# Sums of factor weights moved behind the product of their step, in a fused attention and two-layer kernel on one core

## Chip, core and metric

The kernel runs on one core of a Trainium2 chip. The metric is the device time of one execution in microseconds (us): a median of 858.5 us over three runs (857.91 to 858.9). The profile that is quoted here is of one more execution, which took 857.15 us.

Engines by their names in the profile: PE is TensorE (matmuls; PEld its weight loads), DVE is VectorE, ACT is ScalarE, POOL is GpSimd, SP is SyncE, which here only issues DMAs. Each engine works through its own list of instructions in the order of the program. ACT and POOL issue DMAs from their own lists too.

## The reference

Attention in which a query sees only the keys of its hash bucket, and behind it a layer with a squared ReLU:

```
q_bits, k_bits = (q @ proj > 0), (k @ proj > 0)          # 6 bits: a bucket number
mask   = q_bucket[:, :, :, None] == k_bucket[:, :, None, :]
scores = where(mask, (q @ k.T) / sqrt(64), -1e9)
x      = softmax(scores) @ v                             # 4 x 8 heads, 768 x 64
x      = x as 3072 tokens x 512
out    = max(x @ w_in, 0) ** 2 @ w_out                   # 512 -> 2048 -> 512
```

All in float32.

## The kernel before

**Stages.** The attention comes first, in pairs of heads, up to about 317 us of the profile; beside it the two weight matrices are converted, cut into blocks, and written back to DRAM. What follows is the layer, in three chunks of 1024 tokens. For each chunk there is a hidden stage (`hidden` for the first chunk, `hidden_pair` for the others) and an output stage (`project`). The tokens stand on the free axis, so the hidden values of a chunk are kept in SBUF as five big tiles `b11`, `b12`, `b21`, `b22`, `b_t`.

**Fast matrix products.** Both products of the layer are computed with seven products of half-sized blocks instead of eight (Winograd's form). The blocks of weights enter as sums and differences, prepared once; the blocks of activations as sums and differences made by VectorE (`minus`). The output product is cut twice so: `project` runs over seven outer products, k = 0 to 6, and each is a call of `product` (L828), which does seven inner ones. The chunks after the first also cut three of their seven hidden products once more (`inner_steps`); the weights for this are the *factors* in the DRAM tile `w_in_49`, and they are made while the first chunk is computed.

**One call of `product`** issues seven blocks of four matmuls of 128x256 in the output stage. The weights of each block are a `leaf`, loaded by ACT's queue. Three accumulators in PSUM (`acc0` to `acc2`, two buffers each) take the results. Intermediate states are copied out by ACT (`one`, `two`, `five`, `three`, L844). The finished results are taken by four callbacks `c11`, `c12`, `c22`, `c21`, mostly additions on VectorE (`add_to`, L1201) that read PSUM. Behind the second block stands a `hook` (L1340): it changes a quarter of this product's activations in place (L1342; the seventh block reads the result) and, for some k, makes the activation sums of the next product (`inner_sums`, L1171). In products 4, 5 and 6, finished blocks of the output are transposed on VectorE (`put_out`, L1215) into a tile of the tag `h` and written to the output by four DMAs each, on SyncE's queue or GpSimd's.

**The factors.** `factor_units(n)` (L953), n = 0 to 3, runs in the first chunk's output stage alone, once ahead of each of the products k = 1 to 4:

```
src = [new_h()... for _ in range(2)]          # two tiles, loaded on GpSimd's queue (L957)
sums = [new_h()... for _ in range(2)]         # two tiles, four VectorE instructions (L586 to L589)
...                                           # two stores into w_in_49 on GpSimd's queue (L964)
```

The four VectorE instructions are `sums_a` (L585): one addition and three subtractions of 128x256. The tiles come from `new_h` (L918): `p_r.tile([P, HN], FP32, name="h", bufs=NH)`, with NH = 5 buffers of 128x512 for all tiles of the tag `h`, those of `put_out` among them. A tile takes a buffer when it is asked for, and its first writer waits until whatever used the buffer is done.

**What sets the order.** The layer is written under a manual schedule: on each engine the instructions stand as the code calls them, and waits are put in for data and for buffers. So the place of a call in `project` is the place of its instructions in each engine's list. Between the products stand further sums: after k = 0 and k = 2 two large differences and `inner_sums` (L1367, L1373), after k = 3 and 4 two differences of the next chunk's x (`sum_x`, L1362). On GpSimd's queue the next chunk's x is loaded at k = 0, then come the factors' loads and stores, at k = 5 two pairs of `raw_qk` loads (L879).

Of the kernel before, what the change touches and what calls it, by code (L numbers as in the profile page):

```python
# [34 lines left out]
def kernel(  # L35
# [45 lines left out]
    HF, HD, NR, NQ = DFF // 2, DM // 2, NFF // 2, NFF // 4  # L81
# [503 lines left out]
    def sums_a(a11, a12, a21, a22, s1, s2, s3, s4):  # L585
        nc.vector.tensor_tensor(out=s1, in0=a21, in1=a22, op=ALU.add)  # L586
        nc.vector.tensor_tensor(out=s3, in0=a11, in1=a21, op=ALU.subtract)
        nc.vector.tensor_tensor(out=s2, in0=s1, in1=a11, op=ALU.subtract)
        nc.vector.tensor_tensor(out=s4, in0=a12, in1=s2, op=ALU.subtract)  # L589
# [31 lines left out]
    for pr in range(NIN, NP):  # L621
        n = 16 if pr == NP - 1 else 1 + (pr % 3 == 0)
# [4 lines left out]
    def load_x(i, fs=slice(0, NFT)):  # L627

        if i not in xs:
            x = p_c.tile([P, NFT, NCH], FP32, name="x")  # L630
            xs[i] = x, [p_c.tile([P, 2, NCH // 2], FP32, name=f"t_x{n}") for n in range(3)]
        nc.gpsimd.dma_start(out=xs[i][0][:, fs], in_=x_all[:, fs, i * NCH:(i + 1) * NCH])
# [23 lines left out]
    with tc.manual_schedule():  # L656
# [261 lines left out]
        def new_h():  # L918
            return p_r.tile([P, HN], FP32, name="h", bufs=NH)
# [30 lines left out]

        thirds = {}

        def factor_units(n):  # L953

            src = [new_h().rearrange("p (a f c) -> p a f c", a=2, c=P) for _ in range(2)]
            for j in range(2):
                nc.gpsimd.dma_start(out=src[j], in_=w_in_7[j * NQ + n, :, 5:7])  # L957
            sums = [new_h().rearrange("p (a f c) -> p a f c", a=2, c=P) for _ in range(2)]
            sums_a(
                src[0][:, :, 0], src[0][:, :, 1], src[1][:, :, 0], src[1][:, :, 1],  # L960
                *(sums[j // 2][:, :, j % 2] for j in range(4)),
            )
            for m in range(2):
                nc.gpsimd.dma_start(out=w_in_49[n, :, 0:2, 2 * m:2 * m + 2], in_=sums[m])  # L964
# [232 lines left out]
        def block(t, n):  # L1197
            return t[:, n]

        def add_to(out, one, two):  # L1200
            nc.vector.tensor_tensor(out=out, in0=one, in1=two, op=ALU.add)  # L1201

        def whole(one, two):

            if two is None:
                return one
            t = p_y.tile([P, QN], FP32, name="tmp", bufs=2)
            add_to(t, one, two)
            return t

        def put_out(i, ih, jh, n, o):


            ot = p_r.tile([P, HN], FP32, name="h", bufs=NH)
            nc.vector.transpose(out=ot, in_=o)  # L1215
            m0 = ih * HD + n * P
            at = slice(i * NCH + jh * HN, i * NCH + (jh + 1) * HN)
            for a in range(P // 32):
                queue = nc.gpsimd if (ih, jh) == (1, 1) else nc.sync
                queue.dma_start(  # L1220
                    out=out[at, m0 + a * 32:m0 + (a + 1) * 32].rearrange("(c i) j -> i c j", i=32),
                    in_=ot[a * 32:(a + 1) * 32].rearrange("i (c j) -> i c j", j=32),
                )
# [37 lines left out]
        def project(i):  # L1261

            V, W, U, X = (p_y.tile([P, 4, QN], FP32, name=f"sum{n}") for n in range(4))
            outs = {}

            def out_block(ih, jh, n):

                row, col = n // 2, n % 2
                if (ih, jh, row) not in outs:
                    outs[ih, jh, row] = [p_y.tile([P, HN], FP32, name="o", bufs=NOUT), 0]  # L1270
                o = outs[ih, jh, row]
                return o[0][:, col * QN:(col + 1) * QN]

            def close(ih, jh, n):
                o = outs[ih, jh, n // 2]
                o[1] += 1
                if (i, ih, jh) == (NCHUNK - 1, 1, 0):
                    put = put_last if n == 2 else put_part
                    put(n, o[0][:, n % 2 * QN:(n % 2 + 1) * QN])
                elif o[1] == 2:  # L1280
                    put_out(i, ih, jh, n // 2, o[0])

            def first_(n, one, two):
                if two is None:
                    nc.scalar.copy(out=block(V, n), in_=one)
                else:
                    add_to(block(V, n), one, two)

            def seventh(n, one, two):
                add_to(block(W, n), block(V, n), whole(one, two))  # L1290

            def fifth(n, one, two):
                if two is None:
                    nc.scalar.copy(out=block(U, n), in_=one)
                else:
                    add_to(block(U, n), one, two)

            def third(n, one, two):
                add_to(block(X, n), block(U, n), whole(one, two))
                add_to(block(X, n), block(X, n), block(V, n))  # L1300

            def second(n, one, two):
                add_to(out_block(0, 0, n), block(V, n), whole(one, two))
                close(0, 0, n)

            def sixth(n, one, two):
                t = whole(one, two)
                add_to(out_block(0, 1, n), block(X, n), t)
                close(0, 1, n)
                add_to(block(W, n), block(W, n), t)  # L1310
                add_to(out_block(1, 1, n), block(W, n), block(U, n))
                close(1, 1, n)

            def fourth(n, one, two):
                add_to(out_block(1, 0, n), block(W, n), whole(one, two))
                close(1, 0, n)

            more = i + 1 < NCHUNK
            uses = first_, seventh, fifth, third, second, sixth, fourth
            for k in range(7):  # L1320
                b = OUTER[k][1]
                t1, t2 = tens.pop(k)
                if k == 0 and more:
                    load_x(i + 1)
                if i == 0 and 0 < k <= NQ:
                    factor_units(k - 1)
                if i == 0 and k == NQ + 1:
                    load_peak(0)
                    load_peak(1)
                if k >= 5 and more:  # L1330
                    load_inner(i + 1, 0, (k - 5,))
                at = lambda m, k=k: lambda n: leaves[k, m][:, n]
                bt = {
                    "11": lambda n: b[:, n, 0:QN], "21": lambda n: b[:, NQ + n, 0:QN],
                    "22": lambda n: b[:, NQ + n, QN:HN], "t1": lambda n: t1[:, n],
                    "t2": lambda n: t2[:, n], "t3": lambda n: b[:, n, QN:HN],
                    "t4": lambda n: b[:, NQ + n, 0:QN],
                }

                def hook():  # L1340
                    y21 = b[:, NQ:NR, 0:QN]
                    minus(y21, y21, t2)  # L1342
                    if k + 1 < 7 and k not in (1, 3):
                        inner_sums(k + 1)
                    if k == 6 and more:
                        load_third_inner(i + 1, 0, nc.scalar)
                        sums_inner(i + 1)

                counted = []

                def a_with_load(m, k=k):
                    load_leaf(7 * k + len(counted) + NLEAF - 2)
                    counted.append(m)
                    return at(m)

                use = uses[k]
                product(
                    NQ, QN, a_with_load, bt, lambda *p: use(0, *p), lambda *p: use(1, *p),
                    lambda p: use(2, p, None), lambda *p: use(3, *p), hook,
                    (i, k) == (NCHUNK - 1, 6),  # L1360
                )
                if k in (3, 4) and i + 1 < NCHUNK:  # L1362
                    sum_x(i + 1, 2 * k - 5)
                    sum_x(i + 1, 2 * k - 4)
                if k == 4 and i + 1 == NCHUNK:
                    guard()
                if k == 0:  # L1367

                    for h in range(2):
                        at_h = slice(h * NQ, (h + 1) * NQ)  # L1370
                        minus(b11[:, at_h], b22[:, at_h], b_t[:, at_h])
                    inner_sums(2)
                if k == 2:  # L1373

                    for h in range(2):
                        at_h = slice(h * NQ, (h + 1) * NQ)
                        minus(b_t[:, at_h], b21[:, at_h], b11[:, at_h])
                    inner_sums(4)
# [291 lines left out]
```

## Time and profile before

| what | value |
|---|---|
| median of three runs | 858.5 us (857.91 to 858.9) |
| the profiled execution: its time, its span | 857.15 us, 855.6 us |
| granted clock of TensorE | 0.999 |
| first chunk's output stage | about 413.7 to 498.3 us |
| busy in it: PE, DVE, ACT, POOL | 84.6, 77.1, 11.7, 18.4 us |
| in product 2 alone (437.9 to 450.0): PE, DVE | 12.1, 8.1 us |
| loads of factors (`h<-w_in`, 8): issue to landing | 4.7 to 13.1 us, median 6.7 |
| stores of factors (`w_in<-h`, 8): issue to landing | 3.2 to 6.5 us, median 4.4 |
| output writes (`out_dram<-h`, 88): issue to landing | 1.8 to 5.1 us, median 3.6 |

The span is the time from the first to the last instruction of the profiled execution; its own time holds 1.55 us more. Times inside the profile count from the span's start. A timeline row gives start, length, engine, source line, operation, tiles written and read, shapes; in brackets the idle time of the engine before it and what ended it. A row of the chain gives start and length of a piece of the work that set the end. The profile leaves buffer numbers out of tile names, so `h` stands for all tiles of that tag, `b` for four of the five big ones.

### The profile page before, as it was taken

Reading aid. Unit: us, or ns where it says so; the run is one execution under the profiler, and the core shown is the slowest. Engines: PE = TensorE matmul, PEld = TensorE weight load, DVE = VectorE, ACT = ScalarE, POOL = GpSimd, SP = SyncE. Lnnn points to the kernel's source line nnn. Section 1 sums busy time; section 2 is a strip of 40 time slices with the busy share of each in tenths; the row PEclk is TensorE's granted clock in tenths of the full one; section 3 lists DMA queues with packets and bytes.
Section 4 is the critical chain, followed back from the end, with each engine's and each line's share of the span. In section 5 each row is a group of like instructions: output and inputs, shape, how many; then the busy total and the mean of one; then the engine's idle time right before and its main releaser. Section 6 shows DMA issues by size and latency. Waiting matters only on the chain.

```text
span 855.6 us, 16996 instructions
## 1 busy us (share of the span) xinstructions
PE 847.3 (99%) x6593; PEld 527.2 (62%) x6593; DVE 749.2 (88%) x1026; ACT 402.0 (47%) x752; POOL 167.8 (20%) x281
## 2 busy tenths in 40 slices
PE   8999999999999999999999999999999999999998
PEld 3544444444544444444788865657888765668886
DVE  5899999999999987989889978888889788889776
ACT  5887777788877762222211135554111355541110
POOL 1321111113321100653121121111000211200003
PEclk9999999999999999999999999999999999999999
DMA  9766899879999525999977976437657875335467
GB/s 201 137 146 152 178 183 200 196 165 249 250 230 230 169 69 214 327 319 291 363 240 221 269 182 221 164 114 276 197 150 190 182 245 172 124 119 161 140 174 144
DMA packets 235892, 170.12 MB, mean 199 GB/s; under 512 B 169320, under 2 KB 192944, under 8 KB 235808
## 3 DMA queue, kind: packets, MB, share of 16 engines
q1 hardware_dynamic: 194832, 87.78, 40.8%
q0 software_dynamic: 16512, 42.45, 15.8%
q10 hardware_dynamic: 24464, 38.78, 15.0%
q8 instruction: 53, 0.87, 0.4%
q14 instruction: 31, 0.25, 0.1%
HBM read 127.14 MB, written 41.16 MB: 197 GB/s over the span
## 4 chain that ended last, share of the span: by engine, by line
PE 97%; DMA 1%; DVE 1%; ACT 0%; issue 0%; SPq 0%; ACTq 0%; DVEq 0%
PE acc L837 39%; PE st L429 18%; PE xo L484 15%; PE acc L1099 13%; PE acc L1052 8%; PE tot L533 2%; PE hash L359 1%; DMA out_dram<-h 1%; DMA qk_nat<-in_k_dram 1%; DVE o L1201 0%; DVE h L1215 0%; DVE h L1232 0%; DVE tmp L1201 0%; DVE bits L409 0%; DVE sum L1201 0%; PE xo L359 0%
## 5 line engine op out<-in xcount | busy, mean ns | idle before, releaser
L435 ACT ACTIVATE e<-st 128x768 f32<-128x768 f32 x192 | 155.5, 810 | 58.3 <-PE st L429 55.2
L429 PE MATMUL st<-feat 64*64 64x384 f32 x1536 | 157.4, 483 | 1.0 <-DVE feat L328 1.0
L484 PE MATMUL xo<-e,v_nat 64*64 64x385 f32 (+1 forms) x1520 | 157.1, 483 | 0.0
L837 PE MATMUL acc<-b,leaf 128*128 128x256 f32 x600 | 133.1, 379 | 0.0
L837 PEld LDWEIGHTS acc<-b,leaf 128*128 128x128 f32 x600 | 113.8, 190 | 16.1 <-issue 0.7
L472 DVE TENSOR_TENSOR total<-total,e 128x1536 f32<-128x1536 f32 x64 | 111.7, 1746 | 4.2 <-ACT e L435 2.8
L395 POOL DMA_DIRECT2D bits<-signed x120 | 62.2, 522 | 217.3 <-ACT signed L384 198.8
L484 PEld LDWEIGHTS xo<-e,v_nat 64*64 64x64 f32 (+1 forms) x1520 | 56.3, 133 | 67.4 <-issue 58.9
L1099 PE MATMUL acc<-t_x,w_unit 128*128 128x512 f32 x192 | 91.0, 596 | 0.0
L429 PEld LDWEIGHTS st<-feat 64*64 64x64 f32 x1536 | 56.0, 133 | 39.2 <-issue 33.8
L837 PE MATMUL acc<-t,leaf 128*128 128x256 f32 x336 | 75.9, 379 | 0.0
L837 PEld LDWEIGHTS acc<-t,leaf 128*128 128x128 f32 x336 | 63.8, 190 | 8.7
L914 DVE SCALAR_TENSOR_TENSOR b<-h 128x512 f32<-128x512 f32 x96 | 65.7, 691 | 3.0
L429 PE MATMUL st<-bits 64*64 64x384 bf16 x768 | 64.9, 325 | 0.1
L837 PE MATMUL acc<-x,w_unit 128*128 128x512 f32 x128 | 56.5, 593 | 0.0
L837 PE MATMUL acc<-b_t,leaf 128*128 128x256 f32 x240 | 53.8, 379 | 0.0
L844 ACT COPY two<-acc 128x256 f32<-128x256 f32 (+1 forms) x29 | 12.5, 432 | 87.8 <-PE acc L837 66.1
L1099 PEld LDWEIGHTS acc<-t_x,w_unit 128*128 128x128 f32 x192 | 35.7, 190 | 27.1 <-issue 23.0
L1220 POOL DMA_DIRECT2D out_dram<-h x24 | 15.6, 657 | 182.1 <-DVE h L1215 182.1
L837 PEld LDWEIGHTS acc<-b_t,leaf 128*128 128x128 f32 x240 | 45.6, 190 | 6.2
L844 ACT COPY one<-acc 128x256 f32<-128x256 f32 (+1 forms) x29 | 12.5, 432 | 78.2 <-PE acc L837 59.0
L429 PEld LDWEIGHTS <-bits 64*64 64x64 bf16 x768 | 23.7, 107 | 37.5 <-issue 36.4
(178 smaller groups left out, 1288.3 us busy)
## 6 DMA issues: line engine op xcount, KB each, us to landing
leaf<-w_out ACTq DMA_DIRECT2D x142, 256.0 KB, 3.1
raw<-in_moe_w_in_dram SPq DMA_DIRECT2D x8, 1024.0 KB, 6.8
raw<-in_moe_w_out_dram SPq DMA_DIRECT2D x8, 1024.0 KB, 7.5
w_unit<-w_in SPq DMA_DIRECT2D x16, 512.0 KB, 4.0
w_unit<-w_in SPq DMA_DIRECT2D x8, 896.0 KB, 8.7
w_out<-sums POOLq DMA_DIRECT2D x16, 448.0 KB, 8.2
v_nat<-in_v_dram SPq DMA_DIRECT2D x16, 384.0 KB, 5.2
x_all<-x_t SPq DMA_DIRECT2D x16, 384.0 KB, 3.0
```

Of the source, the lines that this page charges most:

```text
L395: nc.gpsimd.dma_start(out=t[h * D:h * D + NBITS + 1, w, c * HS:(c + 1) * HS], in_=signed[at:at + NBITS + 1, h],)
L429: nc.tensor.matmul(out=st[k * HK:(k + 1) * HK, h, 0:HS], lhsT=src[1][rows, key], rhs=src[0][rows, cut], start=first, stop=not first, skip_ ...
L435: nc.scalar.activation(out=key_of(pr, kt)[:, :, i, 0:HS], in_=st[:, :, 0:HS], func=ACTF.Exp, scale=scale)
L472: nc.vector.tensor_tensor(out=totals[pr], in0=totals[pr], in1=e, op=ALU.add)
L484: return nc.tensor.matmul(out=outs[pr][h * D:(h + 1) * D, c, 0:HS + 1], lhsT=nat[pr, "v_nat"][rows, h, kt * D:(kt + 1) * D], rhs=key_of(pr ...
L533: done = nc.tensor.matmul(out=spares[pr][g * 32:(g + 1) * 32, c2, 0:QS], lhsT=ones[rows], rhs=totals[pr][rows, h, c, c2 * QS:(c2 + 1) * QS ...
L837: nc.tensor.matmul(out=acc[to], lhsT=a(i), rhs=b(i), start=first and i == 0, stop=last and i == n - 1, skip_group_check=True,)
L844: nc.scalar.copy(out=t, in_=acc[of])
L914: nc.vector.scalar_tensor_tensor(out=out, in0=h, scalar=0.0, in1=h, op0=ALU.max, op1=ALU.mult)
L1052: nc.tensor.matmul(out=out, lhsT=w(a), rhs=b, start=start, stop=stop, skip_group_check=True)
L1099: nc.tensor.matmul(out=to, lhsT=w[:, PLACE[a], f], rhs=bt[b](f), start=first and f == 0, stop=last and f == NFT // 2 - 1, skip_group_check ...
L1220: queue.dma_start(out=out[at, m0 + a * 32:m0 + (a + 1) * 32].rearrange("(c i) j -> i c j", i=32), in_=ot[a * 32:(a + 1) * 32].rearrange("i ...
```

## The change

`factor_units` is split. The two loads become `load_factor_units` and stay ahead of the product, where they were. The four instructions on VectorE and the two stores on GpSimd's queue stay in `factor_units`, which is now called behind the product of the same k, ahead of the other sums that stand between the products. The tiles for the sums are asked for at the new place as well.

```diff
-        def factor_units(n):
+        def load_factor_units(n):
 
             src = [new_h().rearrange("p (a f c) -> p a f c", a=2, c=P) for _ in range(2)]
             for j in range(2):
                 nc.gpsimd.dma_start(out=src[j], in_=w_in_7[j * NQ + n, :, 5:7])
+            return src
+
+        def factor_units(n, src):
+
             sums = [new_h().rearrange("p (a f c) -> p a f c", a=2, c=P) for _ in range(2)]
...
                 if k == 0 and more:
                     load_x(i + 1)
-                if i == 0 and 0 < k <= NQ:
-                    factor_units(k - 1)
+                src = load_factor_units(k - 1) if i == 0 and 0 < k <= NQ else None
...
                     (i, k) == (NCHUNK - 1, 6),
                 )
+                if src:
+                    factor_units(k - 1, src)
                 if k in (3, 4) and i + 1 < NCHUNK:
                     sum_x(i + 1, 2 * k - 5)
```

## The prediction

> **What bounds the kernel now.** I read the busy times first, then the chain of work in the stretch that the change touches, then the waits of that stretch, and last the order of VectorE's and SyncE's instructions in it. The busy times:
>
> ```profile
> PE 847.3 (99%) x6593; PEld 527.2 (62%) x6593; DVE 749.2 (88%) x1026; ACT 402.0 (47%) x752; POOL 167.8 (20%) x281
> ```
>
> TensorE is busy 99% of the span, so no other engine can give time back where TensorE does not wait. The stretch of the change is the first output stage, seven products of about 12.09 us each (the `one` copies of L844 start 12.09 us apart), from 413.7 to 498.3 us. In the chain, in order of time, it is one piece, and the next stage joins it without a gap:
>
> ```profile
> 408.89 89.39 PE acc L837 x403
> 498.28 1.72 PE acc L1099 x4
> 500.00 0.86 PE acc L1052 x4
> 500.87 1.98 PE acc L1099 x4
> ```
>
> TensorE does not wait once here. VectorE does, and these are all its waits from 413 to 500 us:
>
> ```profile
> DVE h L586 <- DMA h<-w_in: 4.6, 2, 3.9
> DVE sum L1201 <- PE acc L837: 1.4, 1, 1.4
> ```
>
> So the sums of factors sometimes wait for their own loads (3.95 us in product 2, 0.69 us in product 4), and TensorE does not notice. VectorE's order around product 4's end, with its start times:
>
> ```profile
> 467.59 0.42 DVE L586 TENSOR_TENSOR h<-h 128x256 f32<-128x256 f32 x1 [0.69 <-DMA h<-w_in]
> ...
> 468.72 0.42 DVE L589 TENSOR_TENSOR h<-h 128x256 f32<-128x256 f32 x1
> 469.06 1.22 DVE L592 TENSOR_TENSOR b<-b,t 128x1024 f32<-128x1024 f32 x1
> ...
> 475.43 0.71 DVE L1215 STREAM_TRANSPOSE h<-o 128x512 f32<-128x512 f32 x1
> ...
> 477.28 0.71 DVE L1215 STREAM_TRANSPOSE h<-o 128x512 f32<-128x512 f32 x1
> 477.91 1.18 DVE L592 TENSOR_TENSOR t_x<-x 128x1024 f32<-128x1024 f32 x1
> ```
>
> The reader is to see two `h` tiles born at 475.43 and 477.28: transposed outputs. SyncE writes them out:
>
> ```profile
> 476.17 6.74 SPq L1220 DMA_DIRECT2D out_dram<-h  x8
> ```
>
> Asked one by one, the first tile's four writes are issued at 476.17, 476.57, 477.08 and 477.80 and land 4.7, 4.7, 4.6 and 4.2 us later, the last at 482.0. From 477.91 VectorE runs without a pause to 503.79, and this row of that run matters at the end:
>
> ```profile
> 500.40 0.42 DVE L1201 TENSOR_TENSOR tmp<-acc,two 128x256 f32<-128x256 f32 x1
> ```
>
> It ends at 500.82 and frees the PSUM bank that TensorE writes at 500.87. That margin is nil.
>
> **The change part by part.** Nothing is added or taken away: four times, four subtractions or additions (L586 to L589) of 0.42 us, 1.47 us a set from the first to the next instruction, and two stores on GpSimd's queue move from in front of product k to behind it (k = 1 to 4). The loads keep their place in the program, but stand behind the previous set's stores on GpSimd's queue.
>
> *Product 1.* Without the set in front, the hook's subtraction (L1342, `b<-b,t`) starts at 432.69, not 434.15. Its reader, the seventh block, begins 10.36 us into the product, at 436.1, so a margin of 0.8 us becomes 2.2. Worth nothing: TensorE was not waiting. The set then runs at 438.25, its data long there (loads of 414.66 and 415.23 landed by 428.3). Its stores go from 434.07 to about 439.6, and the next loads from 435.55 and 436.12 to 441.1 and 441.7.
>
> *Products 2 and 3.* VectorE's 3.95 us wait goes. What is late next is TensorE: the hook may overwrite its tile only after the second block (441.3), and the third result is there at 448.25. The second set follows at 448.93. Its loads landed 4.7 to 7.0 us after issue in the three later sets, so by 448.7: just in time. Behind the set stand the two large differences (4.4 us), the next sums (3.5) and product 3's hook, which ends at 448.93 + 1.47 + 4.41 + 3.53 + 1.22 = 459.56. Its reader begins at 460.3. Cost nothing, while that cover of 0.7 us holds. The third set runs at 464.03 (5.69 us after the hook's start at 458.34, the distance from 458.74 to 464.43 before), its loads (451.8, 452.4) landed by 459.4; stores at 465.4, last loads at 466.9 and 467.5, landed by 474.5.
>
> *Product 4, where I see the cost.* The tag `h` has NH = 5 buffers. Before, the set was over before the two transposes asked for theirs. Now two loaded tiles are held through product 4, two transposes take two more, and the set needs two for its sums: six. The built program of the changed kernel shows which is shared: the third sum (L587, tile `sums[1]`) lies where the first transposed tile lay, and VectorE waits before it for the four semaphores of that tile's four output writes. Counted on from 464.03: the set 1.47, two x differences 2.4, hook and inner sums 4.67, then to the first transpose 1.70. It starts at 474.27, 1.16 us earlier than before, and VectorE reaches the third sum at 477.09. The fourth write is issued at 474.27 + 2.37 = 476.64 (its spacing of before; 476.49 with the 2.22 us of the third chunk).
>
> When it lands is bounded from both sides. In the same place of the third chunk, on quiet DMA engines (busy share 0.70 to 0.75), the fourth write took 2.0 us: 478.5. At most I take the 482.0 of before, with no profit from the earlier start. Between them, the second chunk's took 3.9 us, issued next to two leaf loads at a share of 0.64 to 0.76. Here the `one` copy's two leaf loads are issued at 475.9, while the four `raw_qk` loads of 470.44 to 472.08, which crowded the engines before (share 1.03 from 476 to 478), now stand behind the last stores on GpSimd's queue. The second chunk's row is nearest: 476.6 + 3.9 = 480.5. So VectorE stands still for 3.4 us (1.4 to 5.0).
>
> The Trainium skill, DMA: Bandwidth & Descriptors, section "Anatomy of one DMA — SWDGE (gpsimd) path", gives each DMA some 2.0 us of fixed cost, most of it the wait for the write's receipt. By it a 64 KB write would land at 476.5 + 2.15 and the estimate would be 860.4 us, against 862.2 by the rows; the third chunk's 2.0 agrees, this stretch's 4.2 to 4.7 does not.
>
> *What stands behind that wait.* On VectorE: three more of the set's instructions' time (1.13 from the third sum to the next row), then the differences of x, product 5's hook and everything to 503.79. Before, `t_x<-x` started at 477.91; now 480.5 + 1.13 = 481.65, so VectorE is 3.7 us late (1.75 to 5.3) in a run with no pause to recover in. Who waits for it, on TensorE:
> - product 5's seventh block at 484.47 reads the hook's result, before ready at 481.49: margin 3.0, stall 0.7;
> - product 6's seventh block at 496.55, result before at 494.92: margin 1.6, so 2.1 in all;
> - the next stage's matmul at 500.87, margin nil: 3.7 in all.
>
> The lateness passes whole, as one delay and not as three added up. Behind it TensorE runs 97% of the chain, so nothing later takes it back.
>
> *GpSimd's queue.* The last stores go from 468.98 to about 481.6, `raw_qk` loads from 470.44 to about 483. Read at the earliest at 502.51 (L884), landed by some 490: hidden. The output writes on this queue wait for VectorE anyway.
>
> Sum: 0 + 0 + 0 + 3.7. The profiled execution took 857.15 us (span 855.6 and 1.55 around it), so 860.85; it lies 1.35 under the median of 858.5, so against the median **862.2 us**.
>
> **The rivals.**
> - *A longer chain of delays.* Should the second set's loads land after 448.9, it is late itself, and past 0.7 us product 3's seventh block stalls. For: the 13.1 us of the first set's load. Against: that one stood behind a 2 MB load of x. At 13.1 the set starts 5.9 late, TensorE loses 5.1 there, and VectorE enters product 4 0.7 later against it: 862.2 + 5.1 + 0.7 = 868.
> - *Not slower: the output writes are no obstacle.* The place is the third sum at 477.09. If the last write lands by about 476.8, VectorE is no later than before and TensorE never stops: 858.5. For: the set's bubbles are gone. Against: the smallest landing of any output write in the trace is 1.8 us, and the fourth is not issued before 476.4. Between this and 1.7 us of lateness lies what would count as no change.
> - *Faster, because PSUM is emptied sooner.* The Trainium skill, PSUM — Partial Sum Buffer, section "Summary: rules for kernel authors", says to evacuate promptly; here results of product 1 are read up to 1.46 us sooner. The trace lists no wait of TensorE from 413 to 500 us, so the most to gain is the 0.01 us of issue at 500.86: 858.5, not less.
>
> **How the numbers follow.** Two executions of one kernel differ by up to 0.12% here, so 0.2% (1.7 us) is about what a measurement can tell from no change. Forecast (slower by 1.75 to 5.3, so 860.2 to 863.8): 0.80. Longer chain: 0.07. No obstacle, or a wait under 1.7 us: 0.09. Faster by something that I don't see: 0.04. Slower is 0.87, same 0.09, faster 0.04. The range is the forecast's own with the spread of the median, half a microsecond, on both sides: 859.7 to 864.4.
>
> **What would show it.** In the profile after: before L587 of the fourth set an idle time of about 3.4 us, ended by the writes `out_dram<-h`; the first transpose near 474.3; no 3.95 us wait before the second set; TensorE's chain, whole in the table above, broken near 484.5, 496.6 and 500.9 by VectorE, 3.7 us in sum, and the later stages shifted by as much. Wrong it would be if the writes land as fast as on quiet engines (half the cost), if the second set waits for its loads, or if TensorE's gap at 500.87 hides a margin that the chain doesn't show.

## The result and the profile after

The changed kernel takes 861.4 us (median of six runs, 861.04 to 862.77) against 858.2 us of the kernel before (median of six, the three quoted above among them). The ratio is 1.0042, with a 95% interval of 1.0032 to 1.0052: slower by 3.6 us, between 2.7 and 4.5. The profiled execution took 861.75 us, its span is 860.0 us, 4.4 more than before. Ahead of the changed stage its events come 0.33 to 0.34 us later than before (the next chunk's x is loaded at 414.25, not 413.91). Where single times are compared below with "offset taken off", 0.33 us is subtracted.

TensorE's busy time has moved by 0.9 us only, so most of the loss is idle time:

```profile
PE 848.2 (99%) x6593; PEld 529.3 (62%) x6593; DVE 749.5 (87%) x1026; ACT 401.9 (47%) x752; POOL 167.2 (19%) x281
```

VectorE's waits from 413 to 512 us, in the view of who waited for whom:

```profile
DVE h L587 <- DMA out_dram<-h: 3.8, 1, 3.8
DVE sum L1205 <- PE acc L837: 3.3, 2, 1.9
...
DVE b_t L592 <- PE acc L837: 1.6, 1, 1.6
DVE tmp L1205 <- PE acc L837: 1.5, 1, 1.5
```

The wait for the factors' loads is gone, and one wait for output writes has come. Where it stands, in VectorE's order around the end of product 4:

```profile
474.59 0.71 DVE L1219 STREAM_TRANSPOSE h<-o 128x512 f32<-128x512 f32 x1
...
476.44 0.71 DVE L1219 STREAM_TRANSPOSE h<-o 128x512 f32<-128x512 f32 x1
477.07 0.38 DVE L586 TENSOR_TENSOR h<-h 128x256 f32<-128x256 f32 x1
481.29 0.43 DVE L587 TENSOR_TENSOR h<-h 128x256 f32<-128x256 f32 x1 [3.84 <-DMA out_dram<-h]
...
482.43 1.22 DVE L592 TENSOR_TENSOR t_x<-x 128x1024 f32<-128x1024 f32 x1
```

The first transposed tile's four writes are issued at 475.33, 475.73, 476.25 and 476.80, and land after 1.8, 2.0, 3.8 and 4.3 us, the last at 481.1. The third sum of the fourth set starts 0.2 us later. And TensorE, which had not one stop here before, now has three; its timeline (the profile lists each matmul of the program as two, so a block of four has eight):

```profile
486.15 1.97 PE L837 MATMUL acc<-b,leaf 128*128 128x256 f32 x8 [1.40 <-issue]
...
499.58 1.96 PE L837 MATMUL acc<-b_t,leaf 128*128 128x256 f32 x8 [1.11 <-issue]
...
505.43 1.98 PE L1103 MATMUL acc<-t_x,w_unit 128*128 128x512 f32 x4 [1.30 <-DVE tmp L1205]
```

The profile finds no releaser for the first two ("issue"), but VectorE's rows of the two hooks show it:

```profile
484.83 1.22 DVE L592 TENSOR_TENSOR b<-b,t 128x1024 f32<-128x1024 f32 x1
...
498.29 1.18 DVE L592 TENSOR_TENSOR b_t<-b_t,t 128x1024 f32<-128x1024 f32 x1
```

Product 5's hook ends at 486.05, 0.10 us before the first stop's end, and product 6's at 499.47, 0.11 before the second's. The three idle times make 3.81 us in sum. They are counted from modelled ends of the matmuls before; counted from start to start of the same blocks, before and after, the delays are 1.64, 1.34 and 1.30 us. The matmul at 505.43 is 4.2 us later than before, offset taken off.

### The profile page after: what moved, and what is told of

Its sections match the earlier page's. It is cut to its first block, busy times and chain, and to the rows that moved or that the text cites. A ratio compares the mean times of both kernels' runs of the same rounds, so it can differ in the third digit from the quotient of the medians.

```text
span 860.0 us, 16997 instructions
## 1 busy us (share of the span) xinstructions
PE 848.2 (99%) x6593; PEld 529.3 (62%) x6593; DVE 749.5 (87%) x1026; ACT 401.9 (47%) x752; POOL 167.2 (19%) x281
## 4 chain that ended last, share of the span: by engine, by line
PE 90%; DVE 7%; DMA 2%; issue 1%; ACT 0%; SPq 0%; ACTq 0%; DVEq 0%
PE acc L837 33%; PE st L429 18%; PE xo L484 14%; PE acc L1103 13%; PE acc L1056 8%; PE tot L533 2%; PE hash L359 1%; DVE t L592 1%; DMA out_dram<-h 1%; DVE b_t L592 1%; DMA qk_nat<-in_k_dram 1%; DVE b L592 1%; DVE h L1219 1%; DVE o L1205 1%; DVE sum L1205 1%
```

## The experiments

The theory: the whole cost is VectorE's wait, in front of the fourth set's third sum, for the writes of the first transposed tile, whose `h` buffer that sum takes over. The main rival: moving sums behind a product costs in itself, through VectorE's order or through what moves on GpSimd's queue (factor stores, the next loads, `raw_qk`).

**The fourth set alone back in front.**

```diff
                 src = load_factor_units(k - 1) if i == 0 and 0 < k <= NQ else None
+                if src and k == NQ:
+                    factor_units(k - 1, src)
+                    src = None
```

> The changed kernel with the fourth set of sums back in front of product 4; the sets of products 1 to 3 stay behind. Theory (all of the cost is VectorE's wait, ahead of the fourth set's third sum, for the four output writes of the first transposed tile): no wait on output writes, TensorE's chain whole, 858.2 us, ratio to before 1.000 within 0.001. Rival (each moved set costs, by VectorE's order or by its later stores and loads on GpSimd's queue): three quarters of the 3.6 us, 860.9 us, ratio 1.003.

Measured: ratio 1.0061 (1.0045 to 1.0077). Neither expectation came true. There is no wait for output writes, but another in its place; the row of VectorE's timeline in this kernel:

```profile
474.26 0.43 DVE L586 TENSOR_TENSOR h<-h 128x256 f32<-128x256 f32 x1 [4.67 <-DMA h<-w_in]
```

And TensorE's timeline, the seventh block of product 4 and what follows (two shorter stops come later, 0.23 and 1.31 us):

```profile
477.05 5.42 PE L837 MATMUL acc<-b,leaf 128*128 128x256 f32 x24 [3.10 <-issue]
```

With the third set behind product 3 and the fourth in front of product 4, only the two differences of x lie between them. The fourth set's loads stand behind the third's stores on GpSimd's queue, are issued at 468.5 and 469.0, and the last lands at 474.2; VectorE is there at 469.6. Both expectations left that queue out. As a test between theory and rival it is spoiled, and the run in which the fourth set stands inside product 4 takes its place below.

**The fourth set alone behind.** The complement (`if src and k < NQ` in place of `if src and k == NQ` in the lines above).

> The complement: the sets of products 1 to 3 in front as before, the fourth alone behind product 4. Theory: the whole cost, with the wait before the fourth set's third sum of 3.5 to 4.2 us, 861.0 to 861.8 us, ratio 1.0035 to 1.0045. Rival (each set costs): a quarter, 859.1 us, ratio 1.001.

Measured: ratio 1.0037 (1.0024 to 1.0049), as the theory has it. The wait for the output writes is shorter than expected:

```profile
480.92 0.43 DVE L587 TENSOR_TENSOR h<-h 128x256 f32<-128x256 f32 x1 [3.07 <-DMA out_dram<-h]
```

The fourth write took 3.5 us here, not 4.3. Moving the fourth set alone costs nearly all that the change costs; the rival's 1.001 lies outside the interval. In this execution the wait for the second set's loads, which has stayed in front of product 2, is 4.50 us where the kernel before had 3.95, and it stops TensorE in product 3 for 0.37 us; that part of TensorE's three stops (0.37, 0.94 and 1.30) is not of the moved set. More on that below.

**Another buffer.** The order of all engines as in the changed kernel; only the tile's buffer differs.

```diff
-            sums = [new_h().rearrange("p (a f c) -> p a f c", a=2, c=P) for _ in range(2)]
+            own = [new_h(), new_h() if n < NQ - 1 else p_y.tile([P, HN], FP32, name="o", bufs=NOUT)]
+            sums = [t.rearrange("p (a f c) -> p a f c", a=2, c=P) for t in own]
```

> The changed kernel, order and GpSimd queue untouched, but the fourth set's second sums tile is taken from the tag o (output blocks before the transposing) and not from h, so that five h buffers suffice. Theory: the wait before the third sum is gone, VectorE reaches the next stage's first PSUM read no later than before, 858.2 us, ratio 1.000 within 0.001. Rival (later stores and later raw_qk loads on GpSimd's queue, or VectorE's order in itself): 861.4 us, ratio 1.004.

Measured: ratio 1.0003 (0.9994 to 1.0012). In VectorE's timeline the third sum, written to `o`, runs without a wait:

```profile
477.70 0.41 DVE L587 TENSOR_TENSOR o<-h 128x256 f32<-128x256 f32 x1
```

And TensorE's one stop, at the next stage's first product into the freed bank:

```profile
501.83 1.98 PE L1104 MATMUL acc<-t_x,w_unit 128*128 128x512 f32 x4 [0.36 <-DVE tmp L1206]
```

All four sets stand behind their products, VectorE's order is that of the changed kernel, and the cost is gone with the wait. So the order in itself costs nothing that shows. GpSimd's queue is not quite the same: the last stores are issued at 478.75, some 9 us later than in the kernel before but almost 4 us earlier than in the changed kernel, because the set in front of them no longer waits. The next run has them as late as the changed kernel has.

**Something to do during the wait.** The differences of x run ahead of the fourth set.

```diff
-                if src:
+                if src and k < NQ:
                     factor_units(k - 1, src)
                 if k in (3, 4) and i + 1 < NCHUNK:
                     sum_x(i + 1, 2 * k - 5)
                     sum_x(i + 1, 2 * k - 4)
+                if src and k == NQ:
+                    factor_units(k - 1, src)
```

> The changed kernel with the two differences of x, 2.4 us of VectorE, moved from behind the fourth set to in front of it: they run while the output writes are under way. Theory: the wait falls from 3.8 us to about 1.4 (3.84 less 2.40), TensorE's three stops to 1.4 us in sum, all of it late in the chain because the first margin of 3.0 us covers it at product 5: 859.6 us, ratio 1.0017. Rival (the cost is not a matter of VectorE's time behind the wait but of the writes' or loads' traffic): 861.4 us, ratio 1.004.

Measured: ratio 1.0016 (1.0004 to 1.0027), as the theory has it. The wait in VectorE's timeline:

```profile
481.26 0.42 DVE L587 TENSOR_TENSOR h<-h 128x256 f32<-128x256 f32 x1 [1.32 <-DMA out_dram<-h]
```

And in TensorE's timeline the one stop that is left:

```profile
503.00 1.98 PE L1103 MATMUL acc<-t_x,w_unit 128*128 128x512 f32 x4 [1.31 <-DVE tmp L1205]
```

The writes land when they did in the changed kernel (the fourth at 481.0); 2.4 us of VectorE's work now lie under them, and the time gets back about as much, 2.2 us by the two ratios. The last stores are issued at 482.32 and the `raw_qk` loads from 483.77, as in the changed kernel (482.35 and 483.80). So what moved on GpSimd's queue doesn't set the time either: TensorE waits once, for VectorE.

**Lateness without any wait.** The kernel before, and VectorE made late at the same place by work.

```diff
+                if i == 0 and k == 4:
+                    for _ in range(3):
+                        sum_x(i + 1, 3)
                 if k in (3, 4) and i + 1 < NCHUNK:
```

> The kernel before, its sums in front of the products, with one difference of x (t_x2, 1.22 us to the next row, the same value each time) made three times more on VectorE behind product 4: 3.66 us of lateness at the place where the changed kernel waits, without any wait on output writes, and with GpSimd's queue as before. Theory (VectorE's lateness here passes whole to TensorE, by a margin of 3.0 us at product 5, 1.6 at product 6 and none at the next stage): three stops of TensorE, about 0.7, 1.4 and 1.6 us, 3.66 in sum, ratio 1.0043. Rival (part of the changed kernel's cost comes from the writes or the queues, and VectorE's lateness is partly caught up): under 2 us, ratio under 1.0023.

Measured: ratio 1.0046 (1.0032 to 1.0059). TensorE's stops in its timeline:

```profile
461.31 5.42 PE L837 MATMUL acc<-b,leaf 128*128 128x256 f32 x24 [0.40 <-issue]
...
486.11 1.96 PE L837 MATMUL acc<-b,leaf 128*128 128x256 f32 x8 [0.39 <-issue]
...
499.55 1.97 PE L837 MATMUL acc<-b_t,leaf 128*128 128x256 f32 x8 [1.11 <-issue]
...
505.40 1.98 PE L1099 MATMUL acc<-t_x,w_unit 128*128 128x512 f32 x4 [1.30 <-DVE tmp L1201]
```

The last three are the changed kernel's three places, 2.80 us in sum where I had expected 3.66: here VectorE's wait before the fourth set was 0.17 us and not 0.69, which takes 0.5 off its lateness. The first is not of this edit: the wait for the second set's loads was 4.5 us and not 3.95, and the hook behind it came too late for product 3. All four make 3.20 us. So mere work on VectorE, with no wait for writes and with GpSimd's queue as before, costs about as much as the wait, in the same three places; some 0.4 us of the measured time belongs in this execution to the stop in product 3. With one repetition in place of three:

> The same with one repetition, 1.22 us. Theory: the margins of products 5 and 6 cover it, and one stop of TensorE is left, at the next stage's first product into the freed bank, 1.2 us, ratio 1.0014. Rival (a hidden margin there): no stop, ratio 1.000.

Measured: ratio 1.0008 (0.9995 to 1.0021), an interval that holds both expectations. The trace shows 0.49 us at the expected stop and 1.01 us in product 3, where the wait for the second set's loads was 5.1 us this time. In this execution VectorE did not wait ahead of the fourth set, so its lateness is 1.22 less the 0.69 of before, 0.53, near the 0.49. The time alone settles nothing.

**A longer wait.** The first transposed tile is written in eight DMAs of 32 KB.

```diff
-                queue.dma_start(
...
+                dst = out[at, m0 + a * 32:m0 + (a + 1) * 32].rearrange("(c i) j -> i c j", i=32)
+                src = ot[a * 32:(a + 1) * 32].rearrange("i (c j) -> i c j", j=32)
+                step = 16 if (i, ih, jh, n) == (0, 0, 0, 0) else 32
+                for lo in range(0, 32, step):
+                    queue.dma_start(out=dst[lo:lo + step], in_=src[lo:lo + step])
```

> The changed kernel with the first transposed tile of product 4 written by eight DMAs of 32 KB instead of four of 64 KB: the last is issued some 2 us later. Theory: the wait before the fourth set's third sum grows from 3.84 to between 5.3 and 6.0 us, and the time by as much, to 862.9 to 863.6 us, ratio to before 1.006. Rival (the wait is not what sets the time): 861.4 us, ratio 1.004.

Measured: ratio 1.0084 (1.0071 to 1.0097), 865.0 us. More wait makes more time, but both grew beyond what I had written. VectorE's wait, and the first of TensorE's two stops (the other is 0.58 us at the next stage):

```profile
484.24 0.43 DVE L587 TENSOR_TENSOR h<-h 128x256 f32<-128x256 f32 x1 [7.53 <-DMA out_dram<-h]
...
489.09 3.75 PE L837 MATMUL acc<-b,leaf 128*128 128x256 f32 x8 [5.09 <-issue]
```

SyncE issued six of the eight writes by 476.9 and the last two at 479.3 and 481.7, because it first waited for leaf loads (its list of waits from 474 to 486 us has four for `leaf<-w_out`, 5.9 us in sum). The trace has DMAs of SyncE's and of ACT's queue report their landing on the same semaphores: the write of 479.32 waits for the semaphore of a leaf load that landed at 479.31, and then uses it itself. TensorE's stop brought one thing more. The engines' busy time in the stretches around it (columns: length, then PE, PEld, DVE, ACT, POOL, granted clock, DMA share, GB/s):

```profile
484.00:486.00 2.00, 0.00 (x0) 0.00 (x0) 1.73 (x4) 0.00 (x0) 0.71 (x1) 1.00 1.06 294
486.00:488.00 2.00, 0.00 (x0) 0.00 (x0) 1.97 (x3) 0.00 (x0) 2.00 (x5) 0.61 1.05 288
...
490.00:491.00 1.00, 1.00 (x4) 0.74 (x3) 0.96 (x2) 0.00 (x0) 0.00 (x0) 0.50 0.84 276
...
494.00:496.00 2.00, 2.00 (x11) 1.74 (x11) 1.90 (x6) 0.37 (x1) 0.00 (x0) 1.00 0.06 15
```

The granted clock fell to 0.50 at 486.45, while TensorE stood still, and stayed there until 493.28, so that the eight matmuls behind the stop took 3.75 us; behind the changed kernel's 1.40 us stop they took 1.97.

**The sets inside the products.** What the runs pointed to: VectorE waits in products 1 and 2 for the third finished result, about as long as a set lasts, and a set done there is over before the transposes come.

```diff
+                def c11(*p):
+                    use(0, *p)
+                    if src:
+                        factor_units(k - 1, src)
...
-                if src:
-                    factor_units(k - 1, src)
```

> The changed kernel with each set of sums moved into its product, between the reading of the first finished result (c11, at the second block) and the third (c12): there VectorE waits 1.5 us in product 1 and 1.9 us in product 2 of the changed kernel, and the set, 1.47 us, is over before product 4's transposes ask for buffers. Theory: no wait for output writes, none for factor loads, no stop of TensorE in products 1 to 6, 857.5 to 858.2 us, ratio to before 0.9990 to 1.0000. Rival (sums anywhere but in front of the product cost, by the queues or VectorE's order): above 1.002.

Measured: ratio 0.9991 (0.9982 to 1.0000), 857.65 us. By its middle it is better than both kernels, but against the kernel before by 0.1% only, and the interval reaches 1.0000: a gain is not shown. The chain of work is TensorE's alone again, in one piece of 94 us (the view begins at 405) and on into the next stage:

```profile
404.82 94.48 PE acc L837 x415
499.30 1.72 PE acc L1103 x4
```

And the clean form of the first experiment, the sets of products 1 to 3 behind and the fourth inside product 4 (`if src and k == NQ` in the new `c11` above, `if src and k < NQ` behind the product):

> The sets of products 1 to 3 behind their products as in the changed kernel, the fourth alone between c11 and c12 of product 4, where its loads (landed 472 to 473 us) are there before VectorE comes (473.8) and no buffer is shared with a transposed tile. Theory: 858.2 us, ratio 1.000 within 0.001. Rival (each moved set costs): three quarters of 3.6 us, 860.9 us, ratio 1.003.

Measured: ratio 0.9999 (0.9990 to 1.0008). Moving the first three sets behind costs nothing that this measurement shows (0.1% either way). TensorE's one stop, in its timeline, is the same as with the other buffer:

```profile
501.02 1.98 PE L1103 MATMUL acc<-t_x,w_unit 128*128 128x512 f32 x4 [0.35 <-DVE tmp L1205]
```

## Why the prediction was right, point by point

- *What bounds the kernel.* Right: TensorE without a stop had nothing to gain, and every stop of it is a loss.
- *Products 1 to 3.* Right in each place: with the 0.33 us taken off, the first set runs at 438.17 (said 438.25), the third product's hook ends at 459.56 (said 459.56), the third set runs at 464.03 (said 464.03). The second set's loads, issued at 441.0 and 441.6, landed by 447.3, in time. But "the 3.95 us wait goes" was only half of it. VectorE's waits in products 1 to 4 were 4.64 us for loads; now they are 4.91 us for TensorE's results (1.46, 1.56, 1.89). VectorE's idle time moved.
- *The wait in product 4.* The step that carries the prediction, and shown three ways: with another buffer the cost is gone, with 2.4 us of work beneath the wait it is 2.2 us less, with longer writes it is more.
- *Its size.* Said 3.4 us, measured 3.84. The term that was off is the fourth write's landing: 3.9 us from the second chunk's row, 4.3 in fact. With the offset taken off it was issued at 476.47 (said 476.64), so it landed at 480.74 where 480.5 was said, and another 0.2 us passed before VectorE's sum began, which the forecast had not counted. I took the nearest row because the `raw_qk` loads would be out of the way. They were, and still the DMA engines' busy share from 478 to 480 was 1.07 against 1.10 before. The two slow writes are those issued at and behind the `one` copy's two leaf loads (476.21 and 476.62, 256 KB each); in the second chunk too the write just ahead of such a pair is slow (3.9 us) and the one before it is not (2.0 us). That the leaf loads are the reason was not tested by itself. The estimate by the fixed cost of some 2.0 us that the Trainium skill gives (DMA: Bandwidth & Descriptors, section "Anatomy of one DMA — SWDGE (gpsimd) path") held for the first two writes (1.8 and 2.0 us) and not for the two that decide. That section is on DMAs issued from GpSimd, and these four go by SyncE's queue.
- *How it reaches TensorE.* One delay handed on at three margins, as said; the stops were 1.40, 1.11 and 1.30 in place of 0.7, 1.4 and 1.6, in sum 3.81 for 3.7. The split differs for two reasons. VectorE came 4.2 us late and not 3.7, by the landing and the 0.2 us behind it. And the prediction took the starts of the seventh blocks some 0.2 us too late: by the matmuls' own rows they begin at 484.30 and 496.39 in products 5 and 6 (said 484.47 and 496.55), so the margins are 2.8 and 1.5 us and not 3.0 and 1.6. The 97% that the prediction gives for TensorE's share of the chain behind this stage is that of the whole span; from 512 us on it is about 95%, and the delay was not taken back there.
- *The number.* That the medians differ by 3.6 us, and the forecast was 3.7, is partly luck: in the two profiled executions TensorE's delay is 4.2 us.
- *The margin at the next stage.* The text said that VectorE would be no later than before if the last write landed by 476.8. By its own numbers it would still have been 0.3 us late (477.09 + 1.13 against 477.91), and two kernels without the wait (another buffer; the fourth set inside product 4) show that as stops of 0.36 and 0.35 us. The rival was stated a little too kindly; the forecast had the 0.3 us in its sum.
- *The longer chain* did not come in the changed kernel. It exists in the order of the kernel before: where the second set still stood in front of product 2, its wait for loads was 4.5, 4.5 and 5.1 us in three profiles, and TensorE stopped in product 3 for 0.37, 0.40 and 1.01. The profile of before, with 3.95, had just missed it: its hook in product 3 ended at 459.96 and the seventh block began at 460.07, 0.11 us later, which is what lies between hook and block at the stops above, too. So this margin was nil as well. That the sums inside the product do a little better than before, and that the medians of before and after differ by less than the profiles, would fit such stops in some executions of the kernel before; neither is shown.

## What to carry to other kernels

Before work is moved past other users of a rotating pool, count who holds its buffers at the new place: here the sixth tile for five buffers had to wait for a DMA to DRAM, and the engine that waited had everything else queued behind it. A wait of an engine that is not the bottleneck is priced by its length less the smallest margin behind it (here 2.8 us at product 5, 1.5 at product 6 and none at the next stage, so all of the lateness came through). A removed wait buys nothing while another engine is busy without a stop; the cheapest place for filler work is the wait that the engine has anyway.

## What the runs showed of the hardware beyond that

- TensorE's granted clock fell to 0.50 in a stop of 5.09 us, 2.45 us after the modelled end of the last matmul before it, and was 1.00 again 4.2 us after the matmuls began; in a stop of 3.10 us (the fourth set back in front) it stayed at 1.00. The Trainium skill, TensorE: Matmul & The Clock Gate, section "Part 1: The HAM clock gate (the "warmup" mystery)", has the clock halved after at least one idle window of about 3.4 us, windows running freely. The 3.10 us stop agrees with that. The longer one doesn't quite: by the profile's clock records the fall came before 3.4 us of idleness had passed. Why is not shown.
- Output writes on SyncE's queue were held up before their issue by leaf loads from ACT's queue, 3.4 us in two waits in the changed kernel (both for writes of the second transposed tile, which VectorE's wait does not need) and 5.9 in four with split writes. In the trace the DMAs of the two queues share their completion semaphores: in the changed kernel the write of 480.68 waits for that of the leaf load of 476.62, which landed at 480.66.
